# Folding four accumulated rows of squares to two before the norm products, with a third block of output products and closer spacing of the squares, in a fused attention and gated feed-forward kernel

## Chip, cores, metric

The kernel runs on one core of a Trainium2 chip. The metric is the device time of one execution in microseconds (us). TensorE (PE) multiplies matrices and writes to a memory called PSUM; VectorE (DVE) and ScalarE (ACT) work elementwise. In lines of a profile, L88 is line 88 of the kernel's file, and square brackets hold the time that the engine sat idle before an instruction and what ended it.

## The reference, cut to what matters

```python
# q, k, v: 4 batches x 6016 tokens x 256 channels
qn = q / (norm(q, axis=tokens) + 1e-6);  kn = k / (norm(k, axis=tokens) + 1e-6)
a  = softmax(kn^T @ qn / tau)            # 256 x 256 for a batch
x  = v @ a
out = (sigmoid(x @ w_gate) * (x @ w_val)) @ w_out
```

The kernel folds `a` into the weights (G = a @ w_gate, H = a @ w_val) and then runs the feed-forward part over v in chunks of 512 tokens. While batch b is in its feed-forward part, the scores and squares of batch b+1 are done on the side.

## The kernel before

A batch has 12 chunks; each chunk has 12 slots. In a slot TensorE does two gate products and two value products, ScalarE the sigmoid, VectorE the gated product `hT`. The output products of the chunk before are put four to a slot (a mixed slot), or, in chunks 9 and 10, behind the twelve slots as one block of 48 (the code is cut, at `...`):

```python
for ci in range(NCH):
    block = b + 1 < B and ci in (9, 10)
    for f in range(FC):
        glu(b, ci, f)                      # gate, value, sigmoid, hT
        flush()                            # VectorE copies finished output rows
        if prev is not None and not block:
            out_mms(*prev, f * TPC, (f + 1) * TPC)
        for fn, a in side.get((ci, f), ()):
            fn(*a)                         # scores, squares, ... of batch b+1
        ...
    if prev is not None and block:
        for s in range(TPC):
            for fn, a in side.get((ci, FC + s), ()):
                fn(*a)                     # ScalarE/VectorE work hidden in the block
            out_mms(*prev, s * FC, (s + 1) * FC)
            flush()
    ...
```

The squares of a batch are summed by VectorE into `acc`, four rows of 256 bf16 numbers a partition, one for q and one for k. TensorE then sums over the partitions, row by row, in slot 9 of chunk 9:

```python
def norms_mm(b):
    ...
    acc_q, acc_k = s["acc"]
    ...
    norm_mms(ps, (acc_q,), TPC, True, True, (0,))    # 8 products of 1 column
    for u in range(TPC):                             # 4 products of 256 columns
        mm(ps[:, CB:], ones_bf, acc_k[:, u, :], False, u == TPC - 1, ...)
```

The side work is spread over slots, for one group of four token rows after another; `at(slot, ...)` counts slots from the start of the batch:

```python
first, last = (14 if b == 0 else 0), 9 * FC
for g, (t0, nt) in enumerate(groups):
    s0 = first + g * (last - first) // NCH
    ...
    for i, (fn, w) in enumerate(((acc_square, 0), (acc_add, 0), (acc_square, 1), (acc_add, 1))):
        at(s0 + 1 + 2 * i, fn, n, g, w)
```

The value products write to one of two PSUM buffers, and VectorE frees a buffer by doing `hT`. So the value product of slot f + 2 waits for `hT` of slot f.

## Time and profile before

| | before |
|---|---|
| time, median | 831.65 us (6 runs beside the change) |
| span in the trace | 829.8 us |
| TensorE busy | 816.5 us, 98% |
| VectorE busy | 580.9 us, 70% |
| ScalarE busy | 391.0 us, 47% |
| norm products of one batch, by starts | 0.63 us |
| block of 48 output products, by starts | 5.24 us |

Records of matmuls overlap, so durations do not add up: what a matmul costs in the stream is the time from its start to the next one's start. The lines themselves are in the prediction.

### The profile page before, as it was taken

Reading aid. Unit: us, or ns where it says so; the run is one execution under the profiler, and the core shown is the slowest. Engines: PE = TensorE matmul, PEld = TensorE weight load, DVE = VectorE, ACT = ScalarE, POOL = GpSimd, SP = SyncE. Lnnn points to the kernel's source line nnn. Section 1 sums busy time; section 2 is a strip of 40 time slices with the busy share of each in tenths; the row PEclk is TensorE's granted clock in tenths of the full one; section 3 lists DMA queues with packets and bytes.
Section 4 is the critical chain, followed back from the end, with each engine's and each line's share of the span. In section 5 each row is a group of like instructions: output and inputs, shape, how many; then the busy total and the mean of one; then the engine's idle time right before and its main releaser. Section 6 shows DMA issues by size and latency. Waiting matters only on the chain.

```text
span 829.8 us, 13778 instructions
## 1 busy us (share of the span) xinstructions
PE 816.5 (98%) x5210; PEld 503.4 (61%) x5224; DVE 580.9 (70%) x998; ACT 391.0 (47%) x642; POOL 83.2 (10%) x159
## 2 busy tenths in 40 slices
PE   7899999999999999999999999999999999999998
PEld 4546666666666666665576666666566566666666
DVE  6677777777667777777767777777766666666664
ACT  4554444445644444444654444444555444444442
POOL 5532100002110100000210020000000000000000
PEclk9999999999999999999999999999999999999999
DMA  9999723326755543223874453233222323322111
GB/s 209 206 206 185 134 52 90 50 62 128 138 105 104 102 108 60 53 52 82 158 140 99 84 110 78 51 77 65 61 59 64 72 51 83 70 49 70 46 36 71
DMA packets 78739, 77.19 MB, mean 93 GB/s; under 512 B 50768, under 2 KB 55632, under 8 KB 78672
## 3 DMA queue, kind: packets, MB, share of 16 engines
q0 software_dynamic: 23920, 38.81, 28.3%
q1 hardware_dynamic: 54608, 36.97, 17.1%
q8 instruction: 41, 0.67, 0.3%
q10 hardware_dynamic: 144, 0.52, 0.2%
q14 instruction: 26, 0.21, 0.1%
HBM read 78.64 MB, written 24.64 MB: 124 GB/s over the span
## 4 chain that ended last, share of the span: by engine, by line
PE 95%; DMA 3%; issue 0%; POOL 0%; DVE 0%; ACT 0%; POOLq 0%; ACTq 0%
PE ps_o L88 30%; PE ps_gate L88 29%; PE ps_val L88 29%; PE ps_s L88 4%; DMA k_sb<-in_k_dram 3%; PE ps_gh L88 2%; PE ps_n L88 0%; POOL q_sb L97 0%; PE ps_busy L88 0%; DVE hT L411 0%; PE ps_rk L88 0%; DVE x_sb L296 0%; ACT g_sb L410 0%; POOL k_sb L97 0%; ACT e_sb L309 0%
## 5 line engine op out<-in xcount | busy, mean ns | idle before, releaser
L411 DVE TENSOR_TENSOR hT<-ps_val,g_sb 128x512 bf16<-128x512 f32 (+1 forms) x576 | 391.2, 679 | 214.9 <-ACT g_sb L410 209.7
L410 ACT ACTIVATE g_sb<-ps_gate 128x512 bf16<-128x512 f32 (+1 forms) x576 | 338.2, 588 | 386.7 <-PE ps_gate L88 378.4
L88 PE MATMUL ps_gate<-vT,gh_G 128*128 128x512 bf16 (+1 forms) x1152 | 337.7, 375 | 0.6 <-ACT g_sb L410 0.4
L88 PE MATMUL ps_val<-vT,gh_H 128*128 128x512 bf16 (+1 forms) x1152 | 337.5, 375 | 0.1
L88 PE MATMUL ps_o<-w_out_sb,hT 128*128 128x256 bf16 x2256 | 326.2, 273 | 0.0
L88 PEld LDWEIGHTS <-hT 128*128 128x128 bf16 x2256 | 220.7, 98 | 124.8
L88 PEld LDWEIGHTS <-gh_H 128*128 128x128 bf16 x1152 | 112.7, 98 | 131.0 <-issue 0.4
L88 PEld LDWEIGHTS <-gh_G 128*128 128x128 bf16 x1152 | 112.4, 98 | 38.0 <-issue 0.6
L106 POOL DMA_DIRECT2D v_sb<-in_v_dram x48 | 25.6, 533 | 624.1 <-DMA vT<-v_sb 501.2
L437 DVE COPY out_sb<-ps_o 128x256 f32<-128x256 f32 x188 | 77.6, 413 | 13.5 <-PE ps_o L88 13.5
L88 PE MATMUL ps_s<-k_sb,q_sb 128*128 128x256 bf16 x376 | 66.0, 272 | 6.1 <-DMA k_sb<-in_k_dram 4.4
L88 PEld LDWEIGHTS <-q_sb 128*128 128x128 bf16 x376 | 36.6, 98 | 14.7 <-issue 6.8
L215 DVE TENSOR_TENSOR acc<-acc,sq 128x1024 bf16<-128x1024 bf16 (+1 forms) x66 | 44.1, 669 | 0.0
L176 DVE TENSOR_TENSOR sq<-q_sb 128x1024 bf16<-128x1024 bf16 (+2 forms) x44 | 29.3, 667 | 2.6 <-DMA q_sb<-in_q_dram 2.6
L97 POOL DMA_DIRECT2D q_sb<-in_q_dram x48 | 26.5, 551 | 15.2 <-DMA q_sb<-in_q_dram 6.5
L97 POOL DMA_DIRECT2D k_sb<-in_k_dram x48 | 26.3, 547 | 13.8 <-DMA k_sb<-in_k_dram 10.2
L176 DVE TENSOR_TENSOR sq<-k_sb 128x1024 bf16<-128x1024 bf16 (+2 forms) x34 | 22.4, 658 | 0.9 <-ACT sq L174 0.9
L364 ACT ACTIVATE gh_G<-ps_gh,rrow 128x512 bf16<-128x512 f32 x21 | 14.4, 687 | 12.4 <-PE ps_gh L88 8.5
L174 ACT ACTIVATE sq<-k_sb 128x1024 bf16<-128x1024 bf16 (+1 forms) x11 | 11.2, 1018 | 14.7 <-DMA k_sb<-in_k_dram 11.9
L88 PE MATMUL ps_busy<-ones_wide,ones_bf 128*128 128x512 bf16 x57 | 16.1, 408 | 1.7 <-DVE shift L127 1.6
L366 DVE TENSOR_SCALAR gh_H<-ps_gh,rrow 128x512 bf16<-128x512 f32 x22 | 16.4, 743 | 1.6 <-PE ps_gh L88 1.6
L460 DVE TENSOR_TENSOR acc<-acc,sq 128x1024 bf16<-128x1024 bf16 x16 | 11.1, 692 | 5.7 <-ACT sq L174 5.4
(58 smaller groups left out, 114.7 us busy)
## 6 DMA issues: line engine op xcount, KB each, us to landing
out_dram<-out_sb SPq DMA_DIRECT2D x44, 512.0 KB, 2.9
v_sb<-in_v_dram POOLq DMA_DIRECT2D x44, 256.0 KB, 3.9
q_sb<-in_q_dram POOLq DMA_DIRECT2D x43, 256.0 KB, 7.0
k_sb<-in_k_dram POOLq DMA_DIRECT2D x43, 256.0 KB, 7.8
out_dram<-out_sb SPq DMA_DIRECT2D x4, 384.0 KB, 2.5
w_gate<-in_moe_w_gate_dram POOLq DMA_DIRECT2D x3, 256.0 KB, 6.8
w_val<-in_moe_w_val_dram POOLq DMA_DIRECT2D x3, 256.0 KB, 7.4
w_out_sb<-in_moe_w_out_dram POOLq DMA_DIRECT2D x1, 768.0 KB, 12.6
```

Of the source, the lines that this page charges most:

```text
L88: nc.tensor.matmul(out, lhsT=lhsT, rhs=rhs, start=start, stop=stop, **kw)
L97: nc.gpsimd.dma_start(out=tl[:, :nt, :], in_=rows(src, b)[:, t0 : t0 + nt, :])
L106: nc.gpsimd.dma_start(out=v_sb[:, :nt, :], in_=rows(v, b)[:, t0 : t0 + nt, :])
L174: nc.scalar.activation(out=sq[:, :nt, :], in_=src[:, :nt, :], func=ACT.Square)
L176: engine.tensor_tensor(out=sq[:, :nt, :], in0=src[:, :nt, :], in1=src[:, :nt, :], op=ALU.mult)
L215: nc.vector.tensor_tensor(out=acc[:, :nt, :], in0=acc[:, :nt, :], in1=st[b]["sq", w][:, :nt, :], op=ALU.add)
L364: nc.scalar.activation(out=dst, in_=ps, func=ACT.Copy, scale=r)
L366: nc.vector.tensor_scalar(out=dst, in0=ps, scalar1=r, scalar2=None, op0=ALU.mult)
L410: nc.scalar.activation(out=g_sb[:, :n], in_=ps_gate[:, :n], func=ACT.Sigmoid)
L411: nc.vector.tensor_tensor(out=hts[b, ci][:, f, :n], in0=ps_val[:, :n], in1=g_sb[:, :n], op=ALU.mult)
L437: nc.vector.tensor_copy(out=out_sb[:, s, :], in_=ps)
L460: nc.vector.tensor_tensor(out=acc[w], in0=acc[w], in1=sq[w], op=ALU.add)
```

## The change

The intent: replace 8 + 4 norm products of a batch by 4 + 2, by first folding the four rows of `acc` to a pair of bf16 numbers (a high part and a remainder) on VectorE. The folds are to lie in a third block of output products, in chunk 8; so that the sums are ready for it, scores and squares are packed into 8 chunks where they had 9. The diff is cut: unchanged lines between its parts are left out.

```diff
+    def acc_fold(b, w):
+        acc = st[b]["acc"][w]
+        two = attp.tile([P, 2, C], FP32, tag="two", name="two")
+        nc.vector.tensor_tensor(out=two, in0=acc[:, :2, :], in1=acc[:, 2:, :], op=ALU.add)
+        nc.vector.tensor_tensor(out=two[:, 0, :], in0=two[:, 0, :], in1=two[:, 1, :], op=ALU.add)
+        fold = attp.tile([P, 2, C], BF16, tag=f"fold{w}", name="fold")
+        nc.vector.tensor_copy(out=fold[:, 0, :], in_=two[:, 0, :])
+        nc.vector.tensor_tensor(
+            out=fold[:, 1, :], in0=two[:, 0, :], in1=fold[:, 0, :], op=ALU.subtract
+        )
+        st[b].setdefault("fold", []).append(fold)
...
     def norms_mm(b):
-        acc_q, acc_k = s["acc"]
+        fold_q, fold_k = s["fold"]
...
-        norm_mms(ps, (acc_q,), TPC, True, True, (0,))
-        for u in range(TPC):
-            mm(ps[:, CB:], ones_bf, acc_k[:, u, :], False, u == TPC - 1, skip_group_check=True)
+        norm_mms(ps, (fold_q,), 2, True, True, (0,))
+        for u in range(2):
+            mm(ps[:, CB:], ones_bf, fold_k[:, u, :], False, u == 1, skip_group_check=True)
...
-        first, last = (14 if b == 0 else 0), 9 * FC
+        first, last = (14 if b == 0 else 0), 8 * FC
...
         for ci, s, *call in (
+            (8, 2, acc_fold, n, 0),
+            (8, 3, acc_fold, n, 1),
...
-            block = b + 1 < B and ci in (9, 10)
+            block = b + 1 < B and ci in (8, 9, 10)
```

## The prediction

> **What bounds the kernel now.** I read the page first: the busy shares and the chain that ended last.
>
> ```profile
> PE 816.5 (98%) x5210; PEld 503.4 (61%) x5224; DVE 580.9 (70%) x998; ACT 391.0 (47%) x642; POOL 83.2 (10%) x159
> PE 95%; DMA 3%; issue 0%; POOL 0%; DVE 0%; ACT 0%; POOLq 0%; ACTq 0%
> ```
>
> TensorE is 98% busy and 95% of the chain; the other 3% is the loads of the head. Second, the waits of TensorE alone, to see whether any of it lies in the region that the change touches:
>
> ```profile
> PE ps_s L88 <- DMA k_sb<-in_k_dram: 4.4, 8, 1.3
> PE ps_s L88 <- ACT k_sb L130: 1.7, 1, 1.7
> PE ps_busy L88 <- DVE shift L127: 1.6, 1, 1.6
> PE ps_r L88 <- ACT e_sb L309: 0.6, 1, 0.6
> PE ps_gate L88 <- ACT g_sb L410: 0.4, 1, 0.4
> ```
>
> Columns: total us, times, longest. By the chain in order of time all of these lie before about 53 us. After that the matmul stream has no hole, so the time is the sum of matmul spacings: each matmul removed later gives its spacing back, and each hole put in is lost. Third, the norm stage of the second batch in the timeline of TensorE (start, duration of the group, what):
>
> ```profile
> 197.70 0.59 PE L88 MATMUL ps_val<-vT,gh_H 128*128 128x512 bf16 x2
> 198.14 0.34 PE L88 MATMUL ps_n<-ones_bf,acc 128*128 128x1 bf16 x8
> 198.34 0.60 PE L88 MATMUL ps_n<-acc,ones_bf 128*128 128x256 bf16 x4
> 198.77 0.59 PE L88 MATMUL ps_gate<-vT,gh_G 128*128 128x512 bf16 x2
> ...
> 200.50 5.40 PE L88 MATMUL ps_o<-w_out_sb,hT 128*128 128x256 bf16 x48
> 205.74 0.59 PE L88 MATMUL ps_gate<-vT,gh_G 128*128 128x512 bf16 x2
> ```
>
> Read starts, not durations, since groups overlap: eight one-column products from 198.14 to 198.34, 0.20 us; four 256-column products to 198.77, 0.43 us; a block of 48 output products from 200.50 to 205.74, 5.24 us, 109 ns each. Fourth, VectorE in that same block, the place where a new block will put the folds:
>
> ```profile
> 203.32 0.42 DVE L437 COPY out_sb<-ps_o 128x256 f32<-128x256 f32 x1 [0.89 <-PE ps_o L88]
> 203.66 0.22 DVE L238 TENSOR_SCALAR n_sb<-n_sb 128x130 f32<-128x130 f32 x1
> 203.91 0.97 DVE L239 RECIPROCAL n_sb<-n_sb 128x130 f32<-128x130 f32 x1
> 204.80 0.36 DVE L437 COPY out_sb<-ps_o 128x256 f32<-128x256 f32 x1
> 205.07 0.21 DVE L238 TENSOR_SCALAR n_sb<-n_sb 128x128 f32<-128x128 f32 x1
> 205.32 0.95 DVE L239 RECIPROCAL n_sb<-n_sb 128x128 f32<-128x128 f32 x1
> 206.19 0.36 DVE L437 COPY out_sb<-ps_o 128x256 f32<-128x256 f32 x1
> 207.00 0.69 DVE L411 TENSOR_TENSOR hT<-ps_val,g_sb 128x512 bf16<-128x512 f32 x1 [0.45 <-ACT g_sb L410]
> ```
>
> Two inversions of about 1.2 us each go between the copies of the output rows, and VectorE is still 0.45 us early for the first gated product of the next chunk (207.00). That product ends at 207.69; the third value product of that chunk, which needs the freed PSUM buffer, starts at 207.90. So the margin is 0.21 us as executed, and 0.45 + 0.21 = 0.66 us of VectorE work could be added here without a hole in TensorE.
>
> **What the Trainium skill says.** (1) "TensorE: Matmul & The Clock Gate", section "Wait — 56ns, not 53.3ns?": warm matmuls follow each other at N / 2.4 GHz plus about 2.5 ns, with a floor near 25 ns for small N. The trace agrees: 109 ns at 256 columns, 0.20 / 8 = 25 ns at one column. (2) "VectorE: DVE Perf Modes", section "The perf-mode tier table": a two-tensor operation reaches double rate in bf16 only and single rate in fp32, an fp32 copy in SBUF double rate; its errata section gives (N + 151) / 0.96 ns for the fp32 addition. Before has no fp32 addition, but the gated product with one fp32 input is at single rate, (512 + 151) / 0.96 = 691 ns against 691 ns in its group (L411, 128x512), and the cast of 128x1024 f32 to bf16 took 694 ns, which is double rate. (3) Same page, section "The DRAIN you can't avoid": chaining does not shorten a run of operations. In the trace a dependent VectorE operation starts 0.03 us after the end of the one before (L238 to L239), an independent one about 0.08 us before it (L239 to L437), so a chain of four dependent ones is dear for its little work.
>
> **The change part by part.**
>
> *Norm products, removed from TensorE.* Three batches are affected (the first has its own head). q goes from 8 to 4 one-column products: 4 x 25 ns = 0.10 us. k goes from 4 to 2 of 256 columns: 2 x 109 = 0.22 us. Together 0.32 us per batch, all on the path: 0.95 us over three.
>
> *The third block.* In chunk 8 the output products now stand after the twelve gate/value slots instead of four in each. The work is the same: a mixed slot takes 1.30 us (starts of the output groups at 79.31 and 80.61) and a slot in a block 0.863 us (206.60 to 207.47), and 12 x 0.863 + 5.24 = 15.60 = 12 x 1.30. In a block ScalarE needs 0.60 and VectorE 0.69 us per slot of 0.863, so both keep up, as they do now in chunks 9 and 10. Cost nil.
>
> *Scores and squares in 8 chunks instead of 9.* The same instructions, denser. Over a batch VectorE has room (70%). For the second batch one group comes every 82/12 = 6.8 slots instead of 7.8, so in one slot of interest two square operations meet (about 0.6 us each by start spacing). The lag, 0.61 + 1.2 - 1.30 = 0.5 us, is under the slack of a mixed slot: the gated product ends 1.96 us after its slot begins (gate at 185.38, end 187.34) and its buffer is wanted at 2.60 + 0.43 = 3.03 us, so 1.07 us. Cost nil.
>
> *The folds, added to VectorE.* In the built order of instructions, four dependent operations come between the copies of rows 1 and 2 of block 8, and four more between those of rows 2 and 3. One fold: addition of 128x512 with fp32 output, (512 + 151) / 0.96 = 0.69 us; fp32 addition of 128x256, (256 + 151) / 0.96 = 0.42; fp32 to bf16 copy of 256, double rate, (128 + 151) / 0.96 = 0.29; subtraction, single rate, 0.42. Three handoffs at 0.03 and the early start of 0.08 after it: 1.82 + 0.09 - 0.08 = 1.83 us from its start to the next copy (estimates from the page's formula, with the spacings of the trace).
>
> Now lay them on the block's clock, T = start of the 48 output products, taking the copies from the trace: copy of row 1 at T + 2.82, first fold at 3.16, copy of row 2 at 3.16 + 1.83 = 4.99, second fold 0.30 later at 5.29, copy of row 3 at 7.12, first gated product of chunk 9 at 7.46, its end at 8.15. TensorE ends the block at T + 5.24 and wants that buffer for its third value product at T + 7.40 (207.90 - 200.50). With a release of 0.05 us (at 53.10 to 53.15 in the chain) it starts at 8.20: a hole of 0.80 us. By the other way of counting: two folds take 2 x (1.83 - (204.80 - 203.66 = 1.14, or 1.12)) = 1.4 us more than two inversions did, less the 0.66 us of room, plus the release of 0.05: 0.8. After it VectorE, at 0.61 us start to start against 0.863 us a slot, is ahead again by the next product; there is one hole per batch, and TensorE's other waits in the block (the fourth output row needs the copy of row 1) are not touched.
>
> *Sum.* Per batch -0.32 + 0.80 = +0.48 us, over three +1.4: 831.61 + 1.4 = 833.0, and I take 832.9 as some of the hole may be less (a copy after a long operation runs 0.36 instead of 0.42 us).
>
> **The rivals.** (a) *No hole, only the saving*: 831.61 - 0.95 = 830.7. It needs a fold of about 1.43 us instead of 1.83 (the hole is twice the fold less 2.86). For it: VectorE is idle for 30% of the span. Against it: that idle time is not in this stretch, and the formula fits the trace's single-rate product exactly. (b) *A worse hole*: if bf16 inputs with fp32 output, or two fp32 SBUF inputs, are slower than the formula, or the handoffs dearer, by 0.2 us a fold: the hole grows by 0.4 us, and the time is 834.2. (c) *The denser squares or loads bite*: waits of the gated products in chunks 0 to 7 of the first batch, or scores that wait for k. For it: the DMA row of the page is at 7 to 9 tenths in the first slices, and the loads come forward. Against it: the load queue runs chunks ahead and TensorE shows no load wait after the head. It would add 1 to 3 us. (d) *The bound moves to VectorE overall*: it is at 70%, and 24 short operations (11 us in all) make that 71%. No.
>
> **Range and chances.** The saving is safe to 0.1 us. The hole is the uncertain part: 0.3 to 1.1 us a batch, so -0.1 to +2.4 us in all. I take 831.2 to 834.1. Two per cent would be 16.6 us; nothing here is a tenth of that, in either direction: faster by over 2% 0.005, within 2% 0.985, slower 0.01.
>
> **What would show it.** The norm products of one batch should span about 0.32 us by starts instead of 0.63. The waits of TensorE should show a new row, value products waiting for the gated product on VectorE, 3 times, some 0.6 to 0.9 us each, at the third value product of chunk 9. The timeline of VectorE should show eight fold operations of 0.69, 0.42, 0.29, 0.42 us, and no idle time before the first gated product of chunk 9. A block of 48 output products should still be 5.24 us. I am wrong if the new row is missing (rival a), if it lies elsewhere (rival c), or if the holes exceed 1.2 us (rival b).

## The result

| | before | after |
|---|---|---|
| time, median | 831.65 us (831.45 to 831.92, 6 runs) | 834.27 us (834.21 to 835.78, 6 runs) |
| span in the trace | 829.8 us | 832.3 us |
| ratio | | 1.0034, 95% interval 1.0021 to 1.0047 |

A ratio is the mean time of one kernel's runs over that of the other's in the same rounds, so it is not quite the ratio of the two medians. The change costs 2.62 us; predicted was 832.9 us, within 831.2 to 834.1. Within 2% was right, the sign too, but the range was missed.

One caution: 834.21 to 834.35 hold five of the six runs and 835.78 the sixth. Such a longer execution turns up with several kernels (before: 833.06, 833.27 and 833.02 us, at mean granted clocks of TensorE of 0.997 and 0.998). Its cause is open, since none of the longer executions was traced. The clock's mean alone does not mark it: the profiled run of the change, 834.21 us, has 0.998 too. In that trace the clock is 0.83 from 7 to 8 us and 0.62 from 8 to 12 us, and 1.00 elsewhere, so 0.17 + 4 x 0.38 = 1.69 us of clock were lost in the head, where the time is set by loads. The same stretch among dense matmuls would cost about 1.7 us (an estimate from that trace). Medians pass a longer execution by where it is rare, the intervals do not.

First the page of the changed kernel: the busy shares and the chain that ended last (followed back from the last instruction, at each step to what it waited for).

```profile
PE 818.4 (98%) x5206; PEld 503.1 (60%) x5206; DVE 590.9 (71%) x1022; ACT 391.3 (47%) x642; POOL 83.3 (10%) x159
PE 94%; DMA 3%; DVE 1%; issue 0%; ACT 0%; POOL 0%; POOLq 0%; DVEq 0%; ACTq 0%
```

TensorE still reads 98% busy; it is no use for a difference of 0.3%. ("Perfetto Trace Analysis" of the Trainium skill, section "Identifying the Most-Contended Engine", says that matmul busy time is not a good measure of how close TensorE is to its highest rate. This pair of traces agrees: 816.5 us in the faster kernel and 818.4 in the slower, although that one does 18 matmuls fewer. Part of the 1.9 us may be a flaw of the record: before's trace has 5210 matmuls for 5224 weight loads, so 14 are missing.) What is new is the 1% of VectorE in the chain. Next the waits of TensorE (total us, times, longest), those that differ from before:

```profile
PE ps_val L88 <- DVE hT L424: 2.3, 4, 0.7
```

Value products wait for the gated product, four times. The prediction had named this row for three times, one for each batch. The timeline of TensorE shows one of them and then the shorter norm products (start, duration, what):

```profile
191.40 0.59 PE L88 MATMUL ps_gate<-vT,gh_G 128*128 128x512 bf16 x2
192.69 0.59 PE L88 MATMUL ps_val<-vT,gh_H 128*128 128x512 bf16 x2 [0.69 <-DVE hT L424]
...
199.16 0.24 PE L88 MATMUL ps_n<-ones_bf,fold 128*128 128x1 bf16 x4
199.27 0.38 PE L88 MATMUL ps_n<-fold,ones_bf 128*128 128x256 bf16 x2
199.49 0.59 PE L88 MATMUL ps_gate<-vT,gh_G 128*128 128x512 bf16 x2
```

Two gate products take 0.43 us, so the value product was due at 191.83 and came at 192.69: 0.86 us lost. The profile counts only 0.69 as idle, since the record of the matmul ahead (0.59 us for a pair that takes 0.43 by starts) runs on into the gap. The norm products take 0.33 us by starts (199.16 to 199.49) where they took 0.63. VectorE at the same place, the block's rows 1 to 3 and the first gated product of the next chunk:

```profile
187.26 0.42 DVE L450 COPY out_sb<-ps_o 128x256 f32<-128x256 f32 x1 [0.88 <-PE ps_o L88]
187.60 0.68 DVE L223 TENSOR_TENSOR two<-acc 128x512 f32<-128x512 bf16 x1
188.31 0.43 DVE L224 TENSOR_TENSOR two<-two 128x256 f32<-128x256 f32 x1
188.78 0.29 DVE L226 CAST fold<-two 128x256 bf16<-128x256 f32 x1
189.10 0.43 DVE L227 TENSOR_TENSOR fold<-two,fold 128x256 bf16<-128x256 f32 x1
189.44 0.42 DVE L450 COPY out_sb<-ps_o 128x256 f32<-128x256 f32 x1
...
191.62 0.42 DVE L450 COPY out_sb<-ps_o 128x256 f32<-128x256 f32 x1
191.96 1.28 DVE L424 TENSOR_TENSOR hT<-ps_val,g_sb 128x512 bf16<-128x512 f32 x2
```

No idle bracket after the first line: VectorE works without a break, and `hT` comes as soon as the copies are done, too late. The block of 48 began at 184.44, so the first gated product starts 7.52 us after it, against 7.46 in the prediction. Such a hole lies in all three batches (gate at 191.40, 391.74 and 592.09, value at 192.69, 393.04 and 593.38): 0.86, 0.87 and 0.86 us.

Three holes of 0.86 less the saving, 3 x (0.86 - 0.31) = 1.65 us, leaves about 1 us of the 2.62 open. The chain in order of time shows where: besides these, three stretches go through a gated product and a square operation, near 177, 256 and 457 us. The first, in the timeline of TensorE and then of VectorE:

```profile
176.29 0.59 PE L88 MATMUL ps_gate<-vT,gh_G 128*128 128x512 bf16 x2
177.10 0.59 PE L88 MATMUL ps_val<-vT,gh_H 128*128 128x512 bf16 x2 [0.22 <-DVE hT L424]
...
174.96 0.69 DVE L424 TENSOR_TENSOR hT<-ps_val,g_sb 128x512 bf16<-128x512 f32 x1 [0.61 <-ACT g_sb L423]
175.57 0.41 DVE L450 COPY out_sb<-ps_o 128x256 f32<-128x256 f32 x1
175.90 0.55 DVE L215 TENSOR_TENSOR acc<-acc,sq 128x768 bf16<-128x768 bf16 x1
176.36 1.28 DVE L424 TENSOR_TENSOR hT<-ps_val,g_sb 128x512 bf16<-128x512 f32 x2
```

Due at 176.72, came at 177.10: 0.38 us. It is the last addition to `acc` of the second batch, which the packing moved from slot 107 (14 + 86 + 7, in chunk 8) to slot 96 (14 + 75 + 7), the first of the twelve slots ahead of the new block, where a copy sits too and there are no output products to give time. The other two are alike, at slot 9 of the first chunk of the later batches. Before, then after, VectorE there:

```profile
254.10 0.41 DVE L437 COPY out_sb<-ps_o 128x256 f32<-128x256 f32 x1
254.58 0.69 DVE L411 TENSOR_TENSOR hT<-ps_val,g_sb 128x512 bf16<-128x512 f32 x1
255.19 0.68 DVE L176 TENSOR_TENSOR sq<-q_sb 128x1024 bf16<-128x1024 bf16 x1
```

```profile
255.03 0.41 DVE L450 COPY out_sb<-ps_o 128x256 f32<-128x256 f32 x1
255.36 0.68 DVE L176 TENSOR_TENSOR sq<-q_sb 128x1024 bf16<-128x1024 bf16 x1
255.96 1.28 DVE L424 TENSOR_TENSOR hT<-ps_val,g_sb 128x512 bf16<-128x512 f32 x2
...
255.97 0.59 PE L88 MATMUL ps_gate<-vT,gh_G 128*128 128x512 bf16 x2
256.70 0.59 PE L88 MATMUL ps_val<-vT,gh_H 128*128 128x512 bf16 x2
```

Copy and square operation were a gated product apart; now they follow each other (the last two lines are TensorE's). And these slots are short: the chunk before is the batch's last, with three rows of output in place of four, so its 36 output products are done after slot 8, and slots 9 to 11 have none. The next value product starts 0.73 us after its gate product (255.97 to 256.70) in place of 0.43: 0.30 us lost, in each of two batches. The list of waits does not show these: between the records the gap is only 256.70 - (255.97 + 0.59) = 0.14 us, and the smallest gap that the views here list is 0.15 us.

The sum closes. From the last wait of the head (the value product at 53.15 us before, at 52.95 after) to the last run of output products in the chain (821.74 and 824.18 us) it is 768.59 us before and 771.23 after, 2.64 us more. The six holes are 0.86 + 0.87 + 0.86 + 0.38 + 0.30 + 0.30 = 3.57 us, three norm stages give back 3 x 0.31 = 0.93, and 3.57 - 0.93 = 2.64. By starts the change's TensorE has no other hole of 0.1 us there.

### The profile page after: what moved, and what is told of

The parts are those of the page before. It is cut to its first block, busy times and chain, and to the rows that moved or that the text cites. A ratio compares the mean times of both kernels' runs of the same rounds, so it can differ in the third digit from the quotient of the medians.

```text
span 832.3 us, 13781 instructions
## 1 busy us (share of the span) xinstructions
PE 818.4 (98%) x5206; PEld 503.1 (60%) x5206; DVE 590.9 (71%) x1022; ACT 391.3 (47%) x642; POOL 83.3 (10%) x159
## 4 chain that ended last, share of the span: by engine, by line
PE 94%; DMA 3%; DVE 1%; issue 0%; ACT 0%; POOL 0%; POOLq 0%; DVEq 0%; ACTq 0%
PE ps_o L88 30%; PE ps_val L88 29%; PE ps_gate L88 29%; PE ps_s L88 4%; DMA k_sb<-in_k_dram 3%; PE ps_gh L88 3%; DVE hT L424 1%; ACT g_sb L423 0%; DVE out_sb L450 0%; PE ps_n L88 0%; DVE sq L176 0%; PE ps_busy L88 0%; POOL q_sb L97 0%; PE ps_rk L88 0%; DVE x_sb L309 0%
## 5 line engine op out<-in xcount | busy, mean ns | idle before, releaser
L88 PE MATMUL ps_o<-w_out_sb,hT 128*128 128x256 bf16 x2256 | 320.7, 273 | 0.0
```

What stands on the lines that cost most here:

```text
L88: nc.tensor.matmul(out, lhsT=lhsT, rhs=rhs, start=start, stop=stop, **kw)
```

## The experiments

**Theory A**: the 2.62 us are three holes of 0.86 after the folds, plus 0.38 + 0.30 + 0.30 from the closer packing of the squares, less 3 x 0.32 of norm products: 2.58 + 0.98 - 0.96 = 2.60 (with the 0.30 to 0.31 measured in place of 0.32, 2.63). **Theory B**: the folds are the whole of it and the rest is drift. **Theory C**: the third block, or added VectorE work wherever it lies, costs by itself. All kernels gave the right result.

| run | median us (runs) | A foresaw | ratio to before, 95% interval | trace after the head, less before's |
|---|---|---|---|---|
| e1_no_fold | 832.48 (5) | 832.6 | 1.0008, 0.9994 to 1.0022 | +0.95 |
| e2_pack_only | 832.13 (5) | 832.2 | 1.0007, 0.9995 to 1.0020 | +0.58 |
| e3_shift | 833.45 (5) | 833.3 | 1.0019, 1.0006 to 1.0031 | +1.67 |
| e4_spread | 831.76 (5) | 831.7 | 0.9999, 0.9987 to 1.0012 | +0.07 |
| e5_spread_shift | 830.63 (5) | 830.7 | 0.9983, 0.9970 to 0.9997 | -0.90 |
| e6_slots | 830.66 (5) | 830.7 | 0.9983, 0.9971 to 0.9996 | -0.96 |
| e7_long_fold | 839.39 (4) | 838.3 | 1.0088, 1.0074 to 1.0102 | +6.91 |
| e8_bf16_row | 830.36 (5) | 830.2 | 0.9986, 0.9973 to 0.9998 | -1.37 |

All eight ran on the same chip, the first four beside nine runs of before (median 831.65 us), the last four beside nine others (median 831.82 us, two of the nine above 833). The change itself (834.27 us) was not run again beside them. The intervals of e1, e2 and e4 include 1, so their times alone show no difference from before. The last column needs no median: it is the stretch just described in the trace of the profiled run, less that of before (768.59 us). It follows what A foresaw, less 831.65, to 0.05 us in all but e7 (+6.91 where A said +6.65); for the change it is +2.64. In each of these traces the holes that A names are the only ones over 0.1 us by starts after the head.

### e1_no_fold: block and packing stay, folds and shorter products go

```diff
-            (8, 2, acc_fold, n, 0),
-            (8, 3, acc_fold, n, 1),
+        norm_mms(ps, (acc_q,), TPC, True, True, (0,))     # norms_mm as before
```

> The change without the folds and with the long norm products; the third block and the closer spacing of the squares stay. Theory A (the loss is three holes of 0.86 us after the folds plus three smaller ones of 0.38, 0.30 and 0.30 us from the closer spacing, less 0.95 us of norm products): the three large holes go, the three small ones stay, so 831.65 + 0.98 = 832.6. Theory B (the folds are the whole of it, the rest is drift between runs): 831.6. Theory C (a block of output products costs by itself): above 833.

Measured 832.48 us (832.44 to 832.50), 0.83 above before. The interval of the ratio includes 1, since one run of before was 1.4 us long; but all five runs lie above eight of the nine runs of before (831.57 to 831.74). The three large holes are gone from its chain, the three small ones stand. Theory B falls, and so does C as put here (above 833).

### e2_pack_only: before, with the packing alone

```diff
-        first, last = (14 if b == 0 else 0), 9 * FC
+        first, last = (14 if b == 0 else 0), 8 * FC
```

> The kernel before with nothing but the closer spacing of scores and squares (8 chunks, no third block, no folds). Theory A: the hole at the start of the third block of the first batch is gone, since that chunk keeps its output products in each slot; the two holes of 0.30 us at the tenth slot of the first chunk of the second and third batch stay: 831.65 + 0.60 = 832.2. Theory B: 831.6.

Measured 832.13 us (four runs at 831.98 to 832.16, one at 833.77), 0.48 above before. In its trace the value product near 255 us again starts 0.73 us after the gate product (255.05 to 255.78). The same gap stands at 454.85 to 455.58, and there is no third. So packing costs without any block or fold. The 0.35 us from here to e1 fit the 0.38 at the start of the new block: with this packing, the block does cost something, by its first slot.

### e3_shift: the change, with the clashing square operations moved by a slot

```diff
-                at(s0 + 1 + 2 * i, fn, n, g, w)
+                at(min(s0 + 1 + 2 * i + (b > 0 and g == 1), 8 * FC - 1), fn, n, g, w)
```

> The change, with only the clashing square operations moved by one slot (group 1 of the later batches one slot later, the last addition of the first batch one slot earlier). Theory A: the three small holes go, the three large ones stay: 834.27 - 0.98 = 833.3. Theory B: 834.3, unmoved.

Measured 833.45 us (833.14 to 833.61), 0.82 below the change. Its waits of TensorE, where the change had four:

```profile
PE ps_val L88 <- DVE hT L424: 2.1, 3, 0.7
```

The three large ones are left. The edit moves nine VectorE operations: all four of group 1 in each of the two later batches by one slot later, and the last addition of the first batch one slot earlier. Three of the nine were seen to clash. Moving so few gave back most of what was unexplained.

### e4_spread: the change, with the same fold operations spread over rows 1 to 3

```diff
-            (8, 2, acc_fold, n, 0),
-            (8, 3, acc_fold, n, 1),
+            # row, tensor, operation of the fold (0 to 3)
+            (8, 1, acc_fold, n, 0, 0), (8, 1, acc_fold, n, 0, 1),
+            (8, 2, acc_fold, n, 0, 2), (8, 2, acc_fold, n, 0, 3), (8, 2, acc_fold, n, 1, 0),
+            (8, 3, acc_fold, n, 1, 1), (8, 3, acc_fold, n, 1, 2), (8, 3, acc_fold, n, 1, 3),
```

> The change, with the same eight fold operations spread over rows 1 to 3 of the block in place of rows 2 and 3, so that VectorE is done 0.5 us earlier than the next chunk's first gated product needs. Theory A: the three large holes go, the small ones stay: 834.27 - 2.58 = 831.7. Theory C (the extra VectorE work costs wherever it lies, or the block does): above 833.

Measured 831.76 us (831.58 to 831.85): 2.51 below the change with the same VectorE operations. (The edit also gives each fold its own buffer `two`; in the change VectorE never paused for the shared one, by the lines above.) VectorE at the end of that block, the last fold operation, the copy of row 3 and the gated product:

```profile
190.28 0.43 DVE L236 TENSOR_TENSOR fold<-two,fold 128x256 bf16<-128x256 f32 x1
190.62 0.42 DVE L458 COPY out_sb<-ps_o 128x256 f32<-128x256 f32 x1
191.16 0.69 DVE L432 TENSOR_TENSOR hT<-ps_val,g_sb 128x512 bf16<-128x512 f32 x1
```

The block began at 184.66, so the gated product starts 6.50 us after it, as early as before the change (207.00 - 200.50), where the change had 7.52. With its length unchanged, the place of the fold in VectorE's order decides over the 0.86 us a batch. In the old place the length counts too (e7, e8).

### e5_spread_shift: both mends

```diff
+  e4_spread and e3_shift together
```

> The change with both mends: the fold operations spread over rows 1 to 3 and the clashing square operations moved by one slot. Theory A: no hole is left, so the shorter norm products show alone: 831.65 - 0.95 = 830.7. If the two mends disturb each other, it stays at 831 or more.

Measured 830.63 us (830.59 to 830.86), and no value product is left in the waits of TensorE. It beats before by 1.0 us (831.65; by 1.2 against the median of the nine runs beside it, 831.82, two of which are long ones) and the change by 3.6 us. That agrees with the 0.95 us that the shorter products were to give.

### e6_slots: both mends' effect without the third block

Against the change, in short:

```diff
-            block = b + 1 < B and ci in (8, 9, 10)
+            block = b + 1 < B and ci in (9, 10)
+            # fold operations in slots 1, 2, 4, 5 (q) and 7, 8, 10, 11 (k) of chunk 8; squares as in e3_shift
```

> No third block: the same eight fold operations, one to a slot, in the mixed slots of chunk 8, the square operations moved as before. Theory A (only where the VectorE work lies counts, the block has no part in it): 830.7, as with the block and both mends. Theory C (the block is needed to hide the folds, as the change meant): holes in the mixed slots, above 831.5.

Measured 830.66 us, the same as e5. Once the squares are moved, the block is neither of harm nor of use: in mixed slots of 1.30 us, away from the copies, one fold operation a slot disturbs nothing. Theory C falls.

### e7_long_fold: the first addition of each fold done twice

```diff
+        for _ in range(2):
             nc.vector.tensor_tensor(out=two, in0=acc[:, :2, :], in1=acc[:, 2:, :], op=ALU.add)
```

> The change with the first addition of each fold done twice (same result): each fold some 0.65 to 0.70 us longer, two folds a batch, three batches. Theory A: the hole grows by all of it, 3 x 1.35 = 4.1 us: 838.3 (838.0 to 838.5), each of the three large holes about 2.2 us by starts. If some of the hole were hidden elsewhere, less.

Four runs: 838.47, 838.59, 840.20 and 840.39 us, so the median, 839.39, lies between two pairs and the expectation was missed. The profiled one is at 838.59. Its hole, with the gate product ahead of it:

```profile
191.49 0.59 PE L88 MATMUL ps_gate<-vT,gh_G 128*128 128x512 bf16 x2
194.23 0.59 PE L88 MATMUL ps_val<-vT,gh_H 128*128 128x512 bf16 x2 [2.15 <-DVE hT L425]
```

Due at 191.92, so 2.31 us, 1.45 more than in the change; 3 x 1.45 on 834.27 gives 838.6, the profiled time. The two added additions take 0.73 and 0.72 us of the start spacing (187.69 to 189.13 and 190.59 to 192.03, in place of 0.71 and 0.72), and all of it came through; 0.65 to 0.70 had been expected. Why two of the four runs were 1.7 us longer is as open as with the other kernels.

### e8_bf16_row: a fold of two bf16 additions to one row

```diff
-        two = attp.tile([P, 2, C], FP32, tag="two", name="two")
+        two = attp.tile([P, 2, C], BF16, tag="two", name="two")
...
-  addition in fp32, copy to bf16, subtraction: a pair of rows
+        nc.vector.tensor_tensor(out=fold[:, 0, :], in0=two[:, 0, :], in1=two[:, 1, :], op=ALU.add)
...
-        norm_mms(ps, (fold_q,), 2, True, True, (0,))      # and 2 products for k
+        norm_mms(ps, (fold_q,), 1, True, True, (0,))      # and 1 product for k
...
+  square operations moved as in e3_shift
```

> The change with the fold cut to two bf16 additions and one bf16 row (0.42 and 0.29 us, in place of four operations and a pair of rows), in the same place, rows 2 and 3 of the block, the square operations moved. Norm products: two of one column and one of 256 a batch. Theory A: two folds of 0.66 us take less than the two inversions that fit the same place, so no hole, and 3 x (6 x 0.025 + 3 x 0.109) = 1.4 us are saved: 830.2. Accuracy is open: one rounding of the sum to bf16; the sums are in bf16 already.

Measured 830.36 us (three runs at 830.28 to 830.36, two at 831.71 and 831.77). A fold takes 0.42 and 0.29 us, VectorE waits 0.23 us for each copy after it, and there is no hole though the folds lie in rows 2 and 3. It is the fastest kernel by its median, 1.3 us below before's 831.65 and 1.5 below the nine runs beside it; the distance to e5 and e6 is too small and the longer runs too many to rank the three. How much accuracy is left to spare was not measured.

## Why the prediction was right or wrong

- **Norm products**: a saving of 0.32 us a batch foreseen, 0.30 to 0.31 by starts (0.63 less 0.33 or 0.32). Right; e5 and e6 show the whole sum alone, 1.0 us.
- **The third block costs nothing**: right once the squares are moved, by e6 against e5 (830.66 and 830.63 us). With the packing as it was built it is not: the step weighed only sigmoid and gated product against a slot of 0.863 us, and the packing puts an addition to `acc` into the first slot of its chunk, 0.38 us (e1 less e2, 0.35).
- **The folds**: the mechanism, its place and its count were right, and the durations were right to 0.01 us (0.68, 0.43, 0.29, 0.43 against 0.69, 0.42, 0.29, 0.42). The hole was 0.86 and not 0.80 us: the first gated product came 7.52 us after the block's start in place of 7.46, mostly because the copy between the folds took 0.34 us start to start where 0.30 was assumed. That is 0.2 us in all. e4 (moved away) and e7 (made longer) show the cause.
- **Scores and squares in 8 chunks, "Cost nil"**: this is the step that failed. It took the slack of a mixed slot, 1.07 us, for every slot, and worked out the spacing for the second batch alone, not for the later two (8 slots in place of 9), where two of the three small holes lie. In a slot without output products the buffer is wanted at 2 x 0.863 + 0.43 = 2.16 us, and the gated product ends at 1.96 as before: 0.20 us of slack (0.41 near 256 us, where two score products lie between). The prediction had this number in hand, as its margin of 0.21 us after a block, and did not use it here. Such slots lie at the start of the new block and at slots 9 to 11 of the first chunk of a batch, and the packing put square operations next to copies in three of them: 0.38 + 0.30 + 0.30 = 0.98 us, from the traces; e3 gave back 0.82 and e2 alone lost 0.48, e1 0.83.
- **Rivals**: (c), that the denser squares bite, was right in kind and just below its 1 to 3 us, but it looked in chunks 0 to 7 of the first batch, where nothing was lost. (a) and (b) did not come, the formula for VectorE held; that (b) named 834.2 us, almost the measured time, is chance, since its holes were to be 1.2 us and were 0.86.
- **The range** had room for a larger fold hole, not for a second kind of hole: 1.4 predicted + 0.2 + 1.0 = 2.6 us.

## What to carry to other kernels

Where one engine is dense, hidden work on another is free only up to the slack at that very spot: take the deadline of each buffer from the trace for each kind of slot, not for the usual slot alone. A change of spacing moves every operation of a side job, so list the slots where it now meets another one, above all where the dense engine has less to do (block edges, short last chunks). If work has a cost in one place, first try the same work some slots earlier: here that alone was worth 2.5 us.

## What the Trainium skill lacked or had wrong

- "VectorE: DVE Perf Modes", the errata section: it checks (N + 151) / 0.96 ns for the fp32 addition at N = 512 and 2048 only. Here it held at N = 256 too (425 ns measured, 424 computed), and nearly for bf16 inputs with an fp32 output of 128x512 (683 against 691 ns).
- Same page, section "The DRAIN you can't avoid": it has no figure for the handoff between dependent operations. The fold shows 0.03 to 0.04 us from the end of one to the start of the next (187.60 + 0.68 to 188.31), while an independent copy starts 0.09 us before the end of the subtraction ahead of it (189.10 + 0.43 to 189.44).
- "Perfetto Trace Analysis", section "Optimization Strategy", tells to find the gaps between slices of the engine: for matmuls that misses part or all of a hole, as the record of the matmul ahead runs into it. Here 0.86 us lost showed as 0.69 idle, and 0.30 us lost did not show among the waits. Spacing by starts shows both.
- Same page, section "Identifying the Most-Contended Engine": its reason, that pipelined instructions of TensorE look smaller in the trace, is not what these traces show. A matmul of 256 columns is recorded with 273 ns (before, ps_o) and takes 109 ns by starts, so it looks longer.
